# GpSimd's additions wait for the VectorE work that the plan puts ahead of them

## The chip, the cores and the metric

The kernel runs on one core of a Trainium2 chip. The core has five engines that run side by side and meet only through semaphores: TensorE (PE in the profile, PEld for its weight loads), VectorE (DVE), ScalarE (ACT), GpSimd (POOL) and SyncE (SP), which issues most transfers. The metric is the time of one execution on the device, in microseconds (us).

## What is computed

Two stages follow each other. Attention takes 4 batches of 8 heads, 1152 keys and 576 queries (each the mean of two neighbouring ones), 64 wide. A feed-forward layer with a leaky activation follows, 2304 tokens by 512, with 2048 hidden columns.

```python
q_pool = q.reshape(B, H, S // factor, factor, D).mean(axis=3)
scores = scale * np.matmul(q_pool, k.transpose(0, 1, 3, 2))
scores = scores - np.max(scores, axis=-1, keepdims=True)
attn = np.exp(scores)
attn = attn / (np.sum(attn, axis=-1, keepdims=True) + 1e-09)
out = np.matmul(attn, v)
...
h = x @ w_in
g = np.maximum(h, 0.0) + alpha * np.minimum(h, 0.0)
return g @ w_out
```

## The kernel before

**Attention** goes over the heads in 16 pairs (`n` = 0, 2, ... 30). Of a pair, the two heads stand on the two halves of the 128 partitions. The queries are handled in two halves of 288 columns, and for each half the 1152 keys come in nine blocks of 128. For one block TensorE makes the scores of both heads (`scores`, L951: eight matmuls, since q and k are split into a high and a low part, and the negated row maximum is one more product), ScalarE takes the exponential of both (L968) into a tile `p` (named `pa`, 128 x 576), and after the nine blocks TensorE multiplies with the values (`weighted`, L995, 36 records in one run). The row sums need the sum over blocks of the `p` tiles. The nine tiles form two groups, `PARTS[1]` = (0..3) and (4..8), and each group is added up tile by tile at L981. Blocks 6 and 8 (`ADDS[1]`) are added by VectorE, the others by GpSimd; each addition reads two tiles of SBUF and needs the one before it in its group. TensorE then sums over the partitions with a matrix of ones (`sums`, L1017).

While one pair is worked on, TensorE already multiplies q and k of the next (L818 and L825) and VectorE takes the maxima straight out of PSUM (`peaks`, L839, 28 for a pair). VectorE also normalises the results of the pair before (L1054, and L1066 for the low part, twice a pair), makes the low parts of q and k (L691, L699), and converts the weights, which arrive as 64-bit floats (`w_convert`, L409 to L427, and L391).

**The feed-forward layer** uses L479 for all its matmuls: a first sweep over the hidden columns that are ready early (`low_sweep`), and from the end of attention a second over the rest (`high_sweep`).

**The order** of the instructions on each engine is set by a planner, `Scheduler`. Each piece of work is a task with an estimated duration, its needs and a priority; `place` emits the tasks one by one in the planned order of time. Work of VectorE and of GpSimd that has two inputs in SBUF carries `lock=True`: in the plan no two such tasks overlap (`lock_free`), whichever engine they are on. On the chip nothing keeps this. An engine takes its instructions in the planned order and each one waits only for the semaphores of the data that it needs:

```python
if t.lock:
    self.lock_free = at + dur
```

Of the kernel before, what the change touches and what calls it, by code (L numbers as in the profile page):

```python
# [22 lines left out]
PE, ACT, DVE, POOL, SP = range(5)  # L23
# [6 lines left out]
class Buf:  # L30


    def __init__(self, ring=None):
        self.ring, self.t = ring, None
        self.writers, self.users = [], []
        if ring:
            ring.made.append(self)
# [30 lines left out]
class Banks(Ring):  # L68
# [6 lines left out]
    def ready_at(self, place):  # L75
        last = 0
        for bank in place[0]:
            if bank.user is not None:
                for u in bank.user.users:
                    if u.end is None:  # L80
                        return None
                    last = max(last, u.end)
        return last
# [25 lines left out]
class Scheduler:  # L109
# [3 lines left out]
    def __init__(self, col_cost, turn, to_pe, from_pe, slack, dma_fixed):  # L113
        self.tasks, self.ready = [], [[] for _ in range(5)]
        self.free = [0.0] * 5
        self.dma_free = 0.0
        self.now = 0.0
        self.col = 0
        self.lock_free = 0.0
        self.turn = turn  # L120
        self.col_cost, self.to_pe, self.from_pe, self.slack = col_cost, to_pe, from_pe, slack
        self.dma_fixed = dma_fixed
        self.hold = ()

    def add(self, eng, dur, emit, reads=(), writes=(), uses=(), deps=(), prio=0.0, col=0, size=0, kind=None, dma=False, lock=False, fixed=None):
        t = Task()
        t.eng, t.dur, t.emit, t.prio, t.col, t.size, t.kind = eng, dur, emit, prio, col, size, kind
        t.next, t.end, t.avail, t.dma = [], None, None, dma or eng == SP
        t.lock, t.fixed = lock, fixed
        before = set(deps)  # L130
        for b in reads:
            before.update(b.writers)
            b.users.append(t)
        for b in (*uses, *writes):
            b.users.append(t)
        t.takes = [b for b in writes if b.ring is not None]
        for b in writes:
            b.writers.append(t)
        before.discard(t)
        t.deps = list(before)  # L140
        t.left = 0
        for d in t.deps:
            if d.end is None:
                d.next.append(t)
                t.left += 1
        if not t.left:
            self.ready[eng].append(t)
        return t
# [48 lines left out]
    def place(self, at, t):  # L197
        for b in t.takes:
            if b.t is None:
                b.ring.take(b)  # L200
        self.now = at
        t.emit()
        self.ready[t.eng].remove(t)
        dur = t.dur
        if t.eng == PE:
            if t.col != self.col:
                dur += ENTER if t.col else LEAVE
            self.col = t.col
        if t.lock:
            self.lock_free = at + dur  # L210
        self.free[t.eng] = at + dur
        t.end = at + dur
        if t.dma:
            self.dma_free = max(self.dma_free, t.end + 650) + t.size / DMA_RATE
            t.end = self.dma_free
            t.avail = t.end + (self.dma_fixed if t.fixed is None else t.fixed)
        else:
            t.avail = t.end + SYNC
        for n in t.next:
            n.left -= 1  # L220
            if not n.left:
                self.ready[n.eng].append(n)
# [3 lines left out]
def attention_ffn(  # L226
# [87 lines left out]
    nc = tc.nc  # L314
# [15 lines left out]
    def dve(n):  # L330
        return (n + 65) / 0.96

    def act(n, psum=False):
        return n / 1.2 + (50 if psum else 93)
# [13 lines left out]
    DMA_RATE = RATE  # L348
    sch = Scheduler(COL, SF, TO_PE, FROM_PE, (SLP, SLA, SLD, 0, 0), DF)
    add = sch.add  # L350

    def dt(name, shape, dtype):
        return dram.tile(shape, dtype, tag=name, name=name)
# [20 lines left out]
    def w_tiles(f, i, w):  # L374

        if w.ring is None:
            wh[f, i] = hpool[0].tile([P, DMO], F32R, tag=f"wh{f}_{i}", name=f"wh{f}_{i}")
            wl[f, i] = hpool[0].tile([P, DMO], F32R, tag=f"wl{f}_{i}", name=f"wl{f}_{i}")
            return
        flat = flat_of(w, F32R)  # L380
        wh[f, i], wl[f, i] = flat[:, :DMO], flat[:, DMO:2 * DMO]

    def w_split(f, i, mag, prio, ring, left):
        w = Buf(ring)

        def high():
            w_tiles(f, i, w)
            nc.scalar.activation(out=wh[f, i], in_=mag.t, func=AF.Copy)

        def low():  # L390
            nc.vector.tensor_tensor(  # L391
                out=wl[f, i], in0=mag.t, in1=wh[f, i].bitcast(F32), op=ALU.subtract
            )

        t = add(ACT, act(DMO), high, reads=[mag], writes=[w], deps=left, prio=prio)
        add(DVE, dve(DMO), low, reads=[mag], writes=[w], deps=[t], prio=prio, lock=True)
        w_done[f, i] = w

    def w_convert(f, i, prio, release=(), ring=None, left=(), first=()):
        raw, mag, bits = Buf(r_raw), Buf(r_mag), Buf(r_bits)  # L400

        def load():
            nc.sync.dma_start(out=raw.t.rearrange("p n t -> p (n t)"), in_=wt[f, i].bitcast(I32))

        def size():
            nc.scalar.activation(out=mag.t, in_=raw.t[:, :, 1].bitcast(F32), func=AF.Abs)

        def top():
            nc.vector.tensor_scalar(  # L409
                out=bits.t, in0=raw.t[:, :, 1], scalar1=3, scalar2=0x3FFFFFF8,  # L410
                op0=ALU.logical_shift_left, op1=ALU.bitwise_and,
            )

        def tail():
            nc.vector.scalar_tensor_tensor(  # L415
                out=bits.t, in0=raw.t[:, :, 0], scalar=29, in1=bits.t,
                op0=ALU.logical_shift_right, op1=ALU.bitwise_or,
            )

        def sign():  # L420
            nc.vector.scalar_tensor_tensor(
                out=bits.t, in0=raw.t[:, :, 1], scalar=-0x40000000, in1=bits.t,
                op0=ALU.bitwise_and, op1=ALU.bitwise_or,
            )

        def value():
            nc.vector.scalar_tensor_tensor(  # L427
                out=mag.t, in0=mag.t, scalar=F64_TINY, in1=bits.t.bitcast(F32),
                op0=ALU.is_ge, op1=ALU.mult,
            )  # L430

        add(SP, 600, load, writes=[raw], deps=first if f == 0 else (), prio=prio - 1, size=P * DMO * 8)
        t0 = add(ACT, act(DMO), size, reads=[raw], writes=[mag], prio=prio)
        t1 = add(DVE, dve(DMO) * 0.6, top, reads=[raw], writes=[bits], deps=release, prio=prio, lock=True)
        t2 = add(DVE, dve(DMO), tail, reads=[raw], writes=[bits], deps=[t1], prio=prio, lock=True)
        t3 = add(DVE, dve(DMO), sign, reads=[raw], writes=[bits], deps=[t2], prio=prio, lock=True)
        add(DVE, dve(DMO), value, reads=[bits], writes=[mag], deps=[t0, t3], prio=prio, lock=True)
        w_split(f, i, mag, prio, ring, left)

# [639 lines left out]
    with ExitStack() as actx:  # L1079
# [69 lines left out]
        t = add(SP, 600, lambda: nc.sync.dma_start(out=nal, in_=alpha), uses=[], writes=[nal_b], deps=[first_load[0]], prio=3)  # L1149
# [84 lines left out]
```

## Time and profile before

| | |
|---|---|
| median of 3 runs | 842.04 us (840.05 to 842.55) |
| the profiled execution, its time | 839.95 us |
| its span in the profile | 838.2 us |
| TensorE busy (PE) | 825.2 us, 98% |
| VectorE busy | 567.0 us, 68% |
| ScalarE busy | 437.4 us, 52% |
| GpSimd busy | 262.4 us, 31% |
| GpSimd's additions, L981 | 160, 240.5 us |

The shares are averages: attention fills the span to about 440 us, and GpSimd works only there; the second sweep runs from about 501 us to the end.

### The profile page before, as it was taken

To read this page: it belongs to the slowest core of one execution; us is meant where nothing else is said; L and a number is where in the kernel's file an instruction comes from. 1 tells how busy PE (TensorE), PEld (TensorE's weight loads), DVE (VectorE), ACT (ScalarE), POOL (GpSimd) and SP (SyncE) were. 2 spreads that over 40 slices of the span, in tenths; PEclk is the share of its full clock that TensorE was granted. 3 is DMA by queue.
4 is the path that set the end of the run, shared out by engine and by line. 5 is a ranking of instruction groups with operands and counts; after the bars stand their busy time and mean duration, and the time that the engine had idled before them with its cause. 6 is when DMAs were issued, how large, how long until landed. Compare 5 with 4: busy or idle time off the path is not lost.

```text
span 838.2 us, 17447 instructions
## 1 busy us (share of the span) xinstructions
PE 825.2 (98%) x6690; PEld 691.4 (82%) x6690; DVE 567.0 (68%) x1035; ACT 437.4 (52%) x1124; POOL 262.4 (31%) x196
## 2 busy tenths in 40 slices
PE   8999999999999999999999999999999999999997
PEld 8767777676777777776779999998898988988986
DVE  7999999999998988889963799632242232322422
ACT  4657676675766676665754676643232233332321
POOL 5665665565565665654550000000000000000000
PEclk9999999999999999999999999999999999999999
DMA  8234345634354433323233768581330421300301
GB/s 274 58 89 164 82 144 140 197 115 123 87 179 122 122 116 77 83 72 109 69 124 121 248 195 260 177 228 58 91 92 3 120 59 46 91 0 1 91 1 45
DMA packets 67759, 93.71 MB, mean 112 GB/s; under 512 B 20004, under 2 KB 45404, under 8 KB 67676
## 3 DMA queue, kind: packets, MB, share of 16 engines
q1 hardware_dynamic: 65516, 88.18, 33.9%
q0 software_dynamic: 2160, 4.42, 3.6%
q8 instruction: 52, 0.85, 0.4%
q14 instruction: 31, 0.25, 0.1%
HBM read 73.48 MB, written 19.02 MB: 110 GB/s over the span
## 4 chain that ended last, share of the span: by engine, by line
PE 86%; DVE 9%; DMA 2%; issue 1%; ACT 1%; SPq 0%; DVEq 0%; ACTq 0%
PE bank L479 44%; PE bank L951 18%; PE bank L995 15%; PE bank L818 6%; DVE bx L839 3%; PE bank L1017 2%; DMA wraw<-wt 1%; DVE x L1066 1%; DVE pa L981 1%; PE bank L825 1%; PE bank L1129 1%; DMA kk<-kt 1%; DVE pos L515 1%; DVE r L1054 0%; DVE wbits L415 0%
## 5 line engine op out<-in xcount | busy, mean ns | idle before, releaser
L981 POOL TENSOR_TENSOR pa<-pa,pa 128x576 f32<-128x576 f32 x160 | 240.5, 1520 | 155.9 <-ACT pa L968 104.4
L839 DVE TENSOR_REDUCE bx<-bank 128x1 f32<-128x384 f32 (+1 forms) x448 | 214.0, 533 | 22.5 <-PE bank L818 19.9
L968 ACT ACTIVATE pa<-bank 128x288 f32<-128x288 f32 x576 | 199.7, 417 | 25.9 <-PE bank L951 17.4
L951 PE MATMUL bank<-q,k 64*128 64x288 f32 x1728 | 206.2, 311 | 0.8 <-DVE mq L923 0.6
L951 PEld LDWEIGHTS bank<-q,k 64*128 64x128 f32 x1728 | 163.3, 184 | 21.1 <-issue 9.3
L995 PE MATMUL bank<-pa,vv 128*64 128x288 f32 x1152 | 146.8, 409 | 0.0
L995 PEld LDWEIGHTS bank<-pa,vv 128*64 128x64 f32 x1152 | 79.9, 137 | 54.8 <-issue 3.8
L526 DVE TENSOR_TENSOR gw<-gs,gw 128x460 fp32r<-128x460 f32 (+1 forms) x55 | 35.1, 638 | 121.2 <-ACT gw L521 121.2
L951 PE MATMUL bank<-mq,neg 64*128 64x288 f32 x576 | 115.2, 291 | 0.0
L818 PE MATMUL bank<-k,q 64*128 64x384 f32 x384 | 110.1, 362 | 3.5 <-DVE bx L839 2.0
L521 ACT ACTIVATE gw<-gs 128x460 fp32r<-128x460 f32 (+1 forms) x55 | 32.4, 589 | 126.7 <-PE bank L479 115.2
L479 PE MATMUL bank<-wlow,wh 128*128 128x460 f32 (+1 forms) x320 | 93.0, 371 | 0.0
L479 PE MATMUL bank<-gw,wh 128*128 128x460 f32 (+1 forms) x320 | 92.8, 371 | 0.0
L951 PEld LDWEIGHTS bank<-mq,neg 64*128 64x128 f32 x576 | 83.3, 184 | 0.0
L818 PEld LDWEIGHTS bank<-k,q 64*128 64x128 f32 x384 | 62.4, 185 | 16.2 <-DVE bx L839 10.0
L515 DVE SCALAR_TENSOR_TENSOR gs<-gs,nal 128x460 f32<-128x460 f32 (+1 forms) x55 | 38.4, 699 | 52.9 <-ACT gs L510 52.9
L479 PE MATMUL bank<-x,wlow 128*128 128x288 f32 x480 | 66.3, 296 | 0.0
L479 PEld LDWEIGHTS bank<-wlow,wh 128*128 128x128 f32 x320 | 60.0, 188 | 7.1
L479 PE MATMUL bank<-gs,wlow 128*128 128x288 f32 x480 | 65.8, 295 | 0.1
L479 PEld LDWEIGHTS bank<-gw,wh 128*128 128x128 f32 x320 | 60.1, 188 | 6.8
L479 PEld LDWEIGHTS bank<-x,wlow 128*128 128x128 f32 x480 | 64.2, 188 | 1.6 <-issue 1.4
L479 PEld LDWEIGHTS bank<-gs,wlow 128*128 128x128 f32 x480 | 63.9, 188 | 1.4 <-DVE gs L526 0.5
(90 smaller groups left out, 1006.2 us busy)
## 6 DMA issues: line engine op xcount, KB each, us to landing
wraw<-wt SPq DMA_DIRECT2D x32, 512.0 KB
vv<-vt SPq DMA_DIRECT2D x32, 288.0 KB
xs<-x SPq DMA_DIRECT2D x32, 288.0 KB
x<-xs SPq DMA_DIRECT2D x32, 288.0 KB
kk<-kt SPq DMA_DIRECT2D x15, 576.0 KB
r<-rrd SPq DMA_DIRECT2D x64, 72.0 KB
yp<-ys SPq DMA_DIRECT2D x32, 144.0 KB
wlow<-xs SPq DMA_DIRECT2D x16, 288.0 KB
```

Source lines behind the costliest of these rows:

```text
L479: nc.tensor.matmul(out=ps[:, :n], lhsT=w[a, c // DMO][:, c % DMO:c % DMO + P], rhs=lo(hl), start=(first and i == 0), stop=(last and i == 2),)
L515: lambda: nc.vector.scalar_tensor_tensor(out=flat(pos), in0=flat(neg), scalar=nal[:, f:f + 1], in1=flat(pos), op0=ALU.mult, op1=ALU.add),
L521: ACT, act(n), lambda: nc.scalar.activation(out=gs.t[:, 0, :n], in_=flat(pos), func=AF.Copy),
L526: lambda: nc.vector.tensor_tensor(out=gs.t[:, 1, :n], in0=flat(pos), in1=gs.t[:, 0, :n].bitcast(F32), op=ALU.subtract),
L818: nc.tensor.matmul(out=ms.t[:, :JW], lhsT=w.q1.t[d, starts[t]:starts[t] + P], rhs=w.k1.t[d, j * JW:(j + 1) * JW], start=True, stop=True,)
L825: nc.tensor.matmul(out=ms.t[:, :S // 4], lhsT=w.rt.t[d, D - D * u:D - D * u + P], rhs=w.k1.t[d, c:c + S // 4], start=u == 0, stop=u == 1,)
L839: nc.vector.tensor_reduce(out=bx.t[:, at, j:j + 1], in_=ms.t[:, :m], axis=AX.X, op=ALU.max)
L951: nc.tensor.matmul(out=ps.t[i][:, :HQ], lhsT=k.t[d, s] if k else neg[d], rhs=r.t[d, q], start=x == 0, stop=x == len(pairs) - 1,)
L968: lambda ps=ps, p=p, i=i: nc.scalar.activation(out=p.t[:, i], in_=ps.t[i][:, :HQ], func=AF.Exp, scale=SCALE),
L981: lambda a=a, b=p, part=part, e=e: e.tensor_tensor(out=part.t, in0=a.t, in1=b.t, op=ALU.add),
L995: nc.tensor.matmul(out=av.t[i * D:(i + 1) * D, :HQ], lhsT=w.vv[i].t[:, e], rhs=p.t[:, i], start=(e == 0), stop=(e == NC - 1),)
L1017: nc.tensor.matmul(out=ps.t[g * 32:(g + 1) * 32, :HQ], lhsT=ones, rhs=acc[n + g // 2][j].t[:, g % 2], start=j == 0, stop=j == m - 1, tile_ ...
```

## The change

The planner keeps the last VectorE instruction with `lock=True` that it emitted (`port`). When it emits a GpSimd instruction with `lock=True`, it adds a dependence on that one, so that the GpSimd instruction waits for a VectorE semaphore. VectorE gets no wait for GpSimd. The weight conversion's functions now return their instruction, so that they count too. Names, durations and orders in the plan are as before; ten lines are inserted, so L981 is L991 after the change.

```diff
+        self.port, self.after = None, None
...
-        t.emit()
+        made = t.emit()
+        if t.lock and made is not None:
+            if t.eng == DVE:
+                self.port = made
+            elif self.port is not None:
+                self.after(made, self.port)
...
+    sch.after = lambda late, early: tc.add_manual_dep(
+        late.ins, early.ins.name, mybir.DependencyInfo(mybir.DependencyClass.Sync, mybir.DependencyReason.DATA),
+        reason="order on the shared port",
+    )
...
         def low():
-            nc.vector.tensor_tensor(
+            return nc.vector.tensor_tensor(
```

The first place is GpSimd's program in one of the regular pairs (the additions that ran from about 296 to 313 us in the profiled execution). `pa_104<-pa_94,pa_97` adds two tiles of exponentials into a new sum; the brackets name the engines whose semaphores the row waits for. Before:

```order
L981 TENSOR_TENSOR pa_101<-pa_98,pa_99 128x576 [waits Activation_49]
L981 TENSOR_TENSOR pa_101<-pa_101,pa_95 128x576 [waits Activation_49,Pool_49]
L981 TENSOR_TENSOR pa_101<-pa_101,pa_88 128x576 [waits Activation_49,Pool_49]
L981 TENSOR_TENSOR pa_102<-pa_89,pa_90 128x576 [waits Activation_49]
L981 TENSOR_TENSOR pa_102<-pa_102,pa_92 128x576 [waits DVE_49,Activation_49]
L981 TENSOR_TENSOR pa_104<-pa_94,pa_97 128x576 [waits Activation_49]
L981 TENSOR_TENSOR pa_104<-pa_104,pa_100 128x576 [waits Activation_49,Pool_49]
```

The same seven after the change:

```order
L991 TENSOR_TENSOR pa_101<-pa_98,pa_99 128x576 [waits DVE_49,Activation_49]
L991 TENSOR_TENSOR pa_101<-pa_101,pa_95 128x576 [waits Activation_49,Pool_49]
L991 TENSOR_TENSOR pa_101<-pa_101,pa_88 128x576 [waits Activation_49,Pool_49]
L991 TENSOR_TENSOR pa_102<-pa_89,pa_90 128x576 [waits Activation_49]
L991 TENSOR_TENSOR pa_102<-pa_102,pa_92 128x576 [waits DVE_49,Activation_49]
L991 TENSOR_TENSOR pa_104<-pa_94,pa_97 128x576 [waits DVE_49,Activation_49]
L991 TENSOR_TENSOR pa_104<-pa_104,pa_100 128x576 [waits Activation_49,Pool_49]
```

No row moved; the first and the sixth got a wait for VectorE. The sixth waits for this part of VectorE's own program, which is the same before and after (its last instruction, L699, is the one waited for):

```order
L1066 TENSOR_TENSOR x_4110<-r,x_4110 128x288 [waits DMAHW0_49,Activation_49]
L1066 TENSOR_TENSOR x_4114<-r,x_4114 128x288 [waits DMAHW1_49,Activation_49]
L981 TENSOR_TENSOR pa_102<-pa_102,pa_93 128x576 [waits Pool_49]
L691 TENSOR_TENSOR q_4125<-qs,q_3710 128x576 [waits DMASW2_49]
L699 TENSOR_TENSOR k_4135<-kk,k_3756 128x1152
```

Nothing moved there, and VectorE's addition in it still waits for GpSimd.

The second place is the end of attention on GpSimd (about 395 to 418 us), where VectorE also has weights and the first sweep to work on. Before:

```order
L981 TENSOR_TENSOR pa_101<-pa_101,pa_95 128x576 [waits Activation_49,Pool_49]
L981 TENSOR_TENSOR pa_101<-pa_101,pa_88 128x576 [waits Activation_49,Pool_49]
L981 TENSOR_TENSOR pa_102<-pa_89,pa_90 128x576 [waits Activation_49]
L981 TENSOR_TENSOR pa_102<-pa_102,pa_92 128x576 [waits DVE_49,Activation_49]
L981 TENSOR_TENSOR pa_104<-pa_97,pa_100 128x576 [waits Activation_49]
```

After:

```order
L991 TENSOR_TENSOR pa_101<-pa_101,pa_95 128x576 [waits DVE_49,Pool_49]
L991 TENSOR_TENSOR pa_101<-pa_101,pa_88 128x576 [waits DVE_49,Pool_49]
L991 TENSOR_TENSOR pa_102<-pa_89,pa_90 128x576 [waits DVE_49]
L991 TENSOR_TENSOR pa_102<-pa_102,pa_92 128x576 [waits DVE_49,Activation_49]
L991 TENSOR_TENSOR pa_104<-pa_97,pa_100 128x576 [waits DVE_49]
```

Here all five in a row wait for VectorE, and where ScalarE's name went away, the VectorE instruction itself stands behind that piece of ScalarE's work.

## Rows read from the trace of the kernel before

**Rows 1.** Busy us of each engine (instructions) in two stretches; then PEclk, DMA share, GB/s.

```profile
200.00:250.00 50.00, 48.76 (x497) 35.37 (x497) 48.69 (x88) 32.19 (x91) 28.19 (x21) 1.00 0.44 130
250.00:300.00 50.00, 50.00 (x540) 38.13 (x537) 42.55 (x85) 33.60 (x94) 30.20 (x23) 1.00 0.38 109
```

**Rows 2.** The chain that ended last, in order of time: start us, us, what.

```profile
58.17 4.52 PE bank L995 x36
...
72.17 1.59 DVE x L1066
...
84.72 4.52 PE bank L995 x36
...
109.88 4.52 PE bank L995 x36
...
123.20 1.96 DVE x L1066 x2
...
135.51 4.54 PE bank L995 x36
...
148.88 2.04 DVE x L1066 x2
...
161.59 4.52 PE bank L995 x36
...
187.12 4.52 PE bank L995 x36
...
202.55 2.15 DVE x L1066 x2
204.70 1.88 DVE pa L981
...
214.67 4.59 PE bank L995 x36
...
290.21 4.52 PE bank L995 x36
...
315.07 4.52 PE bank L995 x36
...
382.28 1.90 DVE pa L981
...
473.44 5.34 DMA wraw<-wt
```

**Rows 3.** L479 alone in a stretch: busy us (instructions) of PE and PEld.

```profile
50.00:380.00 330.00, 0.00 (x0) 0.00 (x0) 1.00 0.41 118
```

**Rows 4.** Timeline of VectorE, 300 to 312 us: start us, us, instructions.

```profile
305.01 2.23 DVE L1066 TENSOR_TENSOR x<-r,x 128x288 fp32r<-128x288 f32 x2
307.17 0.75 DVE L981 TENSOR_TENSOR pa<-pa,pa 128x576 f32<-128x576 f32 x1
...
308.51 1.34 DVE L699 TENSOR_TENSOR k<-kk,k 128x1152 fp32r<-128x1152 f32 x1
```

**Rows 5.** Timeline of GpSimd, 300 to 322 us; idle time before a row in brackets.

```profile
303.94 2.99 POOL L981 TENSOR_TENSOR pa<-pa,pa 128x576 f32<-128x576 f32 x2 [1.85 <-ACT k L684]
310.28 4.32 POOL L981 TENSOR_TENSOR pa<-pa,pa 128x576 f32<-128x576 f32 x3 [3.35 <-ACT pa L968]
```

**Rows 6.** Groups of VectorE's instructions by line, 440 to 838 us: busy us, mean ns.

```profile
L1066 DVE TENSOR_TENSOR x<-r,x 128x288 fp32r<-128x288 f32 x2 | 0.9, 458 | 0.3 <-ACT x L1061 0.2
```

**Rows 7.** The same view of VectorE, 20 to 250 us.

```profile
L839 DVE TENSOR_REDUCE bx<-bank 128x1 f32<-128x384 f32 (+1 forms) x267 | 127.3, 533 | 5.8 <-PE bank L818 4.3 <-PE bank L825 0.6
```

**Rows 8.** What TensorE waited for, 50 to 250 us: us in total, times, longest.

```profile
PE bank L818 <- DVE bx L839: 1.7, 3, 0.7
```

**Rows 9.** The same, 370 to 440 us.

```profile
PE bank L1017 <- DVE pa L981: 1.1, 1, 1.1
```

**Rows 10.** Timeline of GpSimd, 393 to 440 us.

```profile
401.58 3.28 POOL L981 TENSOR_TENSOR pa<-pa,pa 128x576 f32<-128x576 f32 x2 [1.42 <-ACT pa L968]
412.32 14.84 POOL L981 TENSOR_TENSOR pa<-pa,pa 128x576 f32<-128x576 f32 x9 [7.46 <-DVE pa L981]
```

More of the change, by code (lines that the diff above doesn't have):

```diff
@@ L408, in top @@
         def top():
-            nc.vector.tensor_scalar(
+            return nc.vector.tensor_scalar(
                 out=bits.t, in0=raw.t[:, :, 1], scalar1=3, scalar2=0x3FFFFFF8,
@@ L414, in tail @@
         def tail():
-            nc.vector.scalar_tensor_tensor(
+            return nc.vector.scalar_tensor_tensor(
                 out=bits.t, in0=raw.t[:, :, 0], scalar=29, in1=bits.t,
@@ L420, in sign @@
         def sign():
-            nc.vector.scalar_tensor_tensor(
+            return nc.vector.scalar_tensor_tensor(
                 out=bits.t, in0=raw.t[:, :, 1], scalar=-0x40000000, in1=bits.t,
@@ L426, in value @@
         def value():
-            nc.vector.scalar_tensor_tensor(
+            return nc.vector.scalar_tensor_tensor(
                 out=mag.t, in0=mag.t, scalar=F64_TINY, in1=bits.t.bitcast(F32),
```

## Prediction

> **What bounds the kernel now.** I read the busy times by stretch first. From 200 to 250 us TensorE is busy 48.76 of 50 us and VectorE 48.69; from 250 to 300 us TensorE is busy all 50 and VectorE 42.55 [rows 1]. So TensorE is the bound, but in the first half of attention VectorE runs level with it and now and then holds it up. In neither is GpSimd near full (28.19 and 30.20).
>
> The chain in order of time shows where VectorE holds TensorE up. The run of 36 value matmuls (L995) comes twice a pair, so I take one start a pair as a clock: 58.17, 84.72, 109.88, 135.51, 161.59, 187.12, 214.67, then 290.21 three pairs on, and 315.07 [rows 2]. The last step, 24.86 us, is a pair that TensorE alone bounds. All pairs here hold the same matmuls, for nothing of the first sweep runs between 50 and 380 us [rows 3]. The steps before are longer by 1.69, 0.30, 0.77, 1.22, 0.67 and 2.69 us, and the three to 290.21 (75.54 us) by 0.96 together: 8.3 us in all. That is the most that a freer VectorE can give there.
>
> What makes VectorE late is in the same rows. L1066 takes 0.458 us where GpSimd is idle [rows 6]; on the chain one costs 1.59, and pairs of them 1.96, 2.04 and 2.15 instead of 0.92. An L981 of VectorE costs 1.88 and 1.90 [rows 2] instead of 0.75 [rows 4]. These are collisions: the instruction has begun but stands until a GpSimd addition is through, which takes 4.32/3 = 1.44 us [rows 5]. The maxima do not collide: 267 of them average 0.533 us in the stretch where GpSimd is busy more than half the time [rows 7], and one that stood behind an addition would show over 1.
>
> **What the change removes.** Each step of it that costs or gives something:
>
> 1. In a regular pair GpSimd's second addition of the two that end at 306.93 [rows 5] starts among VectorE's two L1066 (2.23 us instead of 0.92 from 305.01 on) and then VectorE still has L981, L691 and L699 to do, to 308.51 + 1.34 = 309.85 [rows 4]. After the change this addition waits for L699. What follows L699 on VectorE are maxima, which do not collide, so the addition runs beside them. VectorE's collision of about 2.23 - 0.92 = 1.3 us goes away but for the 0.2 us or so by which the first L1066 still meets the addition before, so about 1.1.
>
> 2. The addition itself then starts near 309.85 - 1.1 = 308.75 instead of before 306.93 - 1.4, some 3.2 us later, and ends near 310.2. GpSimd's next addition started at 310.28 after 3.35 us of idle time, since it waits for ScalarE [rows 5]. So the delay costs nothing as long as VectorE does lose its collision: the idle time covers it. Without that cover it would end at 311.3, 1.0 us late. Queued behind it are the next additions and a query load on GpSimd's queue; TensorE's row sums and a free `pa` tile wait for these.
>
> 3. In the steady pairs nothing comes of it, because TensorE is the bound there [rows 1]. It counts where VectorE is on the chain. I give each pair the smaller of its collisions and its excess over 24.86: the pair from 58.17 has 1.59 - 0.46 = 1.13 (excess 1.69), so 1.13; the one from 109.88 has 1.96 - 0.92 = 1.04, but an excess of 0.77 only; that from 135.51 has 2.04 - 0.92 = 1.12; that from 187.12 has 2.15 - 0.92 + 1.88 - 0.75 = 2.36; the others have no collision on the chain: 0. Together 5.4 us [rows 2].
>
> 4. At 382.28 the row sums wait for a collided L981 (1.90 - 0.75 = 1.15); TensorE stood idle 1.1 us for it [rows 9]. That 1.1 goes too.
>
> 5. The new waits themselves: where one binds, it is counted in step 2. For one that is already fulfilled the nearest row is the three additions from 310.28, the last two of which carry two waits each and still follow every 1.44 us [rows 5]. So I take 0; if one cost 0.1 us, two or three in a pair would take 0.3 us of an engine that is idle some 20 of 50 us [rows 1], which hides it. No transfer, no matmul and no order changes.
>
> **The sum**: 5.4 + 1.1 = 6.5 us. From below, what is certain to be VectorE's doing is TensorE's own idle time: 1.7 us for maxima from 50 to 250 us [rows 8] and 1.1 later, 2.8 together. From above it is all excess, 8.3 + 1.15 = 9.45. I take 6.5, since the chain names the collided instructions one by one and pipelined matmuls hide part of a stall from the idle time. The profiled execution took 839.95 us, so it would come to 833.5, and 830.5 to 837.2 by the bounds. The three runs shown have a median of 842.04, 2.1 above; the profiled one is the fastest of the four. I add 0.5 for that: 834.0.
>
> **A rule weighed against this.** The Trainium skill, in "SBUF — State Buffer", "Who interferes with whom", says that VectorE and GpSimd share a pair of ports as an exclusive lock, that whoever issues first has it for the whole instruction, that a VectorE instruction with two SBUF inputs contends with a GpSimd one that reads SBUF, and that `tensor_reduce` on trn2 never does. The trace agrees: 1.9 us against 0.75, and 0.533 for the maxima. By the same rule a lock only changes hands: what VectorE no longer waits, someone else must, and a moved addition can meet the next VectorE instruction. That is the first rival.
>
> **Rivals.**
>
> *The collision only moves (or the gain is given back).* VectorE gets no wait for GpSimd, so an addition that is let go late can stand in the way of VectorE instructions behind the one it waited for. Then VectorE loses the same 1.1 us a little later and the sum is 0: about 840 to 841.5. For it: in the first half weight conversions lie between the maxima and will be hit now and then. Against it: of 230 us in that stretch 127.3 are maxima [rows 7], and the plan puts the additions over these. A second way to the same end: the weight loads are on the chain later (5.34 us at 473.44 [rows 2]); if their start did not move forward with attention, the gain would end there. I think it does, since they follow instructions that move too.
>
> *The held additions make things late.* Each pair has a held addition; if VectorE runs as late as before, GpSimd falls 1.0 us behind (step 2), VectorE's own addition of that group waits for it, and all maxima queue behind. Over 15 pairs this is 15 us: 855, or 848 with the gain kept. It decides where an addition is held more than the idle time behind it (3.35 us in the steady pair) beyond its old start plus VectorE's recovery. The end of attention is nearest: five in a row wait there, with 7.46 us of idle time after 401.58 + 3.28 = 404.86 [rows 10]. Against it: ScalarE, which fills the `pa` tiles, is what GpSimd itself waits for in most of its idle time.
>
> *The change does nothing*, because the waits were already implied by the data: excluded for the additions shown, which ran before the instruction they will wait for; I put it with the first rival.
>
> **How the numbers follow.** My forecast (a gain of 2.8 to 9.5 us on the profiled run): 0.74. Collision moves or the gain is given back: 0.15. Late additions: 0.08. A larger gain, if VectorE's head start also takes pairs below 24.86 us: 0.03. A measurement of this kernel can tell about 0.3%, 2.5 us, as the three runs show. Faster by more than that: 0.77, from the forecast (0.72 of its 0.74) and the larger gain, and a little of the rest. Within: 0.15. Slower: 0.08. The forecast alone gives 830.5 to 837.2; to leave no more than 2 in 10 out, the range goes to 840.5, into the first rival, and down to 830.
>
> **What the profile after would show.** If right: L1066 near 0.5 us on average, as in [rows 6]; no L981 of VectorE over 1.5 us at 204 or 382; the six steps of the L995 clock before 214 us, 156.5 us together, down to about 151, and the last unchanged at 24.86; VectorE less busy from 50 to 250 us; GpSimd's idle time put down to VectorE instead of ScalarE. Step 2 is wrong if TensorE or ScalarE waits for GpSimd's L981. The first rival shows as collisions that move to L421, L427, L391 and L415 with the total unchanged. The prediction fails if pairs keep their 25.5 us although the collisions are gone: then something else than the port made VectorE late.

## The result and the profile after

The changed kernel took 831.35 us (median of 5 runs, 830.55 to 833.7), the kernel before, on the same chip, 840.53 us (5 runs, 839.66 to 842.55): a ratio of 0.989, with a 95% interval of 0.9873 to 0.9906, so 9.2 us less. The forecast was 834.0, with a range of 830.0 to 840.5.

The profiled execution after is the longest of its five, 833.7 us with a span of 831.9; it and one more (833.0) had a mean granted clock of 0.997, the other three (830.55 to 831.35) one of 0.998 or 0.999. Its page, busy time by engine and then the chain by engine:

```profile
PE 820.7 (99%) x6690; PEld 691.5 (83%) x6690; DVE 545.4 (66%) x1035; ACT 437.2 (53%) x1124; POOL 250.4 (30%) x196
...
PE 91%; DMA 3%; DVE 3%; ACT 1%; issue 1%; SPq 0%; POOL 0%; DVEq 0%; ACTq 0%; POOLq 0%
```

VectorE has fallen from 9% of the chain to 3%, and TensorE has risen from 86% to 91%. Groups by line, over the whole span, with the idle time ahead of each:

```profile
L991 POOL TENSOR_TENSOR pa<-pa,pa 128x576 f32<-128x576 f32 x160 | 228.7, 1449 | 174.9 <-ACT pa L978 58.0 <-DVE k L709 24.7 <-DVE wbits L425 13.3
...
L991 DVE TENSOR_TENSOR pa<-pa,pa 128x576 f32<-128x576 f32 x64 | 50.2, 784 | 15.5 <-POOL pa L991 15.5
...
L1076 DVE TENSOR_TENSOR x<-r,x 128x288 fp32r<-128x288 f32 x32 | 15.3, 511 | 1.4 <-ACT x L1071 1.1
```

L1076 is the old L1066: 511 ns on average instead of 990, near the 458 ns that it takes where GpSimd is idle [rows 6]. ScalarE's exponentials were named for 104.4 us of GpSimd's idle time before and are for 58.0 now; most of the rest now stands against VectorE's instructions. Busy time by stretch (PE, PEld, DVE, ACT, POOL, then the granted clock):

```profile
20.00:25.00 5.00, 3.41 (x39) 2.66 (x39) 5.00 (x10) 4.31 (x11) 4.59 (x3) 1.00 0.72 178
25.00:30.00 5.00, 5.00 (x45) 4.42 (x42) 3.93 (x9) 3.51 (x10) 2.04 (x2) 0.66 0.00 0
...
200.00:250.00 50.00, 49.99 (x529) 37.33 (x527) 47.85 (x94) 34.14 (x99) 29.60 (x22) 1.00 0.45 130
250.00:300.00 50.00, 50.00 (x539) 38.51 (x537) 41.23 (x85) 34.18 (x94) 30.43 (x23) 1.00 0.39 109
```

From 200 to 250 us TensorE is busy 49.99 us instead of 48.76 [rows 1]. The first two stretches show a loss at the start, told below. The chain in order of time:

```profile
33.85 4.54 PE bank L1005 x36
...
60.40 4.51 PE bank L1005 x36
...
71.98 0.64 PE bank L961 x8
72.89 4.52 PE bank L1005 x36
...
86.06 4.52 PE bank L1005 x36
...
110.36 4.52 PE bank L1005 x36
...
135.29 4.56 PE bank L1005 x36
...
160.44 4.52 PE bank L1005 x36
...
185.38 4.52 PE bank L1005 x36
...
210.92 4.59 PE bank L1005 x36
...
285.73 4.52 PE bank L1005 x36
...
310.43 4.52 PE bank L1005 x36
...
359.84 4.52 PE bank L1005 x36
...
389.16 4.51 PE bank L1005 x36
...
426.11 4.52 PE bank L1005 x36
```

Four starts of the same clock before, which [rows 2] do not have:

```profile
31.23 4.58 PE bank L995 x36
...
364.81 4.52 PE bank L995 x36
...
395.40 4.52 PE bank L995 x36
...
432.69 4.52 PE bank L995 x36
```

The value matmuls (L1005, before L995) are the clock again; the collided L1066 ahead of the second of them [rows 2] is gone, TensorE's own work stands there. The first run starts at 33.85, 2.62 us later than before (31.23). From there on it gains: at 60.40 it is 2.23 us later than before, at 135.29 0.22 earlier, at 210.92 3.75, at 285.73 4.48, at 310.43 4.64, and at 426.11 6.58 (before 432.69). From its first value matmuls on, attention thus won 2.62 + 6.58 = 9.2 us. The medians differ by as much, the two profiled executions (839.95 and 833.7) by 6.25 only: the late start took the difference back.

Two timelines, each by the windows that the text speaks of. VectorE:

```profile
21.19 2.03 DVE L1162 TENSOR_SCALAR nal<-nal 128x16 f32<-128x16 f32 x1
...
300.53 1.02 DVE L1076 TENSOR_TENSOR x<-r,x 128x288 fp32r<-128x288 f32 x2
301.48 0.74 DVE L991 TENSOR_TENSOR pa<-pa,pa 128x576 f32<-128x576 f32 x1
...
302.81 1.34 DVE L709 TENSOR_TENSOR k<-kk,k 128x1152 fp32r<-128x1152 f32 x1
```

And GpSimd:

```profile
21.47 3.19 POOL L991 TENSOR_TENSOR pa<-pa,pa 128x576 f32<-128x576 f32 x2
...
299.45 1.41 POOL L991 TENSOR_TENSOR pa<-pa,pa 128x576 f32<-128x576 f32 x1 [1.83 <-ACT k L694]
304.30 5.82 POOL L991 TENSOR_TENSOR pa<-pa,pa 128x576 f32<-128x576 f32 x4 [3.43 <-DVE k L709]
...
400.62 1.42 POOL L991 TENSOR_TENSOR pa<-pa,pa 128x576 f32<-128x576 f32 x1 [1.86 <-DVE pos L525]
403.84 1.41 POOL L991 TENSOR_TENSOR pa<-pa,pa 128x576 f32<-128x576 f32 x1 [1.80 <-DVE gs L536]
```

This is the regular pair of [rows 4] and [rows 5], 4.5 us earlier. The two L1076 take 1.02 us instead of 2.23. The held addition starts at 304.30, as soon as L709 is through (302.81 + 1.34), and three more follow it without a gap. At the end of attention the additions are let go one by one.

### The profile page after: what moved, and what is told of

Same layout as the page of the kernel before. It is cut to its first block, busy times and chain, and to the rows that moved or that the text cites. A ratio compares the mean times of both kernels' runs of the same rounds, so it can differ in the third digit from the quotient of the medians.

```text
span 831.9 us, 17471 instructions
## 1 busy us (share of the span) xinstructions
PE 820.7 (99%) x6690; PEld 691.5 (83%) x6690; DVE 545.4 (66%) x1035; ACT 437.2 (53%) x1124; POOL 250.4 (30%) x196
## 4 chain that ended last, share of the span: by engine, by line
PE 91%; DMA 3%; DVE 3%; ACT 1%; issue 1%; SPq 0%; POOL 0%; DVEq 0%; ACTq 0%; POOLq 0%
PE bank L489 42%; PE bank L961 21%; PE bank L1005 17%; PE bank L828 6%; PE bank L1027 2%; DMA wraw<-wt 2%; PE bank L835 1%; DMA kk<-qt 1%; DVE pos L525 1%; PE bank L1139 1%; DMA x<-xs 1%; DVE wbits L425 0%; DVE bx L849 0%; DVE gs L536 0%; DVE wmag L437 0%
## 5 line engine op out<-in xcount | busy, mean ns | idle before, releaser
L991 POOL TENSOR_TENSOR pa<-pa,pa 128x576 f32<-128x576 f32 x160 | 228.7, 1449 | 174.9 <-ACT pa L978 58.0
L1005 PE MATMUL bank<-pa,vv 128*64 128x288 f32 x1152 | 146.8, 409 | 0.0
L1005 PEld LDWEIGHTS bank<-pa,vv 128*64 128x64 f32 x1152 | 79.9, 137 | 54.9 <-issue 3.8
L828 PE MATMUL bank<-k,q 64*128 64x384 f32 x384 | 107.4, 359 | 1.7 <-ACT k L766 1.3
```

The lines of the kernel that those rows point to most:

```text
L828: nc.tensor.matmul(out=ms.t[:, :JW], lhsT=w.q1.t[d, starts[t]:starts[t] + P], rhs=w.k1.t[d, j * JW:(j + 1) * JW], start=True, stop=True,)
L991: lambda a=a, b=p, part=part, e=e: e.tensor_tensor(out=part.t, in0=a.t, in1=b.t, op=ALU.add),
L1005: nc.tensor.matmul(out=av.t[i * D:(i + 1) * D, :HQ], lhsT=w.vv[i].t[:, e], rhs=p.t[:, i], start=(e == 0), stop=(e == NC - 1),)
```

## The experiments

**The theory:** the gain is VectorE's, which no longer stands behind GpSimd's additions; each place at which it did gives its part. **The rivals:** the gain comes from one place alone or from the weight conversions; any order between the two engines would do; without the change's wait a collision that is taken away only moves to the next instruction. The kernel before was timed again beside the experiments, on the same chip each time: 840.73 us for the first four below (15 runs), 839.67 for the one with two instructions freed and for the last (9 runs), 840.05 for the other four (23 runs). The value-matmul clock is given relative to the trace of before, plus for later and minus for earlier.

**Where the gain lies: the wait on the first 91 of GpSimd's instructions only (up to about 240 us).**

```diff
-            elif self.port is not None:
-                self.after(made, self.port)
+            else:
+                self.held += 1
+                if self.port is not None and self.held <= 91:
+                    self.after(made, self.port)
```

> The waits stand only on GpSimd's first 91 two-input instructions, those up to about 241 us of the profile before; the rest run as before. Theory (the gain is VectorE no longer standing behind GpSimd in the pairs where VectorE holds TensorE up, 8.3 of it before 290 us and 1.15 near 382): all but about 1.2 us of the gain stays, so 832 to 833.5 against 840.5 before, and the chain has the collided L981 near 382 back. Rival (the gain comes from the end of attention, where five additions in a row are held, or from GpSimd being held anywhere, evenly over the pairs): about half the gain, 836.

834.36 us (834.02 to 835.45), ratio 0.9928 (0.9914 to 0.9941); 832 to 833.5 was missed, since the rest is worth more than the 1.2 us put down for it. The clock goes from +0.1 to -6.3 us at 240 us and then stays at -6.3 to the end. The profile shows TensorE's wait for VectorE's sum (now L1030, of [rows 9]) again, 1.1 us. So 6.4 us are won in the first half of attention, one us more than the terms of the sum for it, and nothing is lost later.

**The other part, `self.held > 91`.**

> The waits stand only on the additions after the 91st, from about 246 us on. Theory: the pairs from 250 to 370 us are bound by TensorE at 24.86 us and gain nothing although their L1066 collisions go; 1.2 us is won near 382; so 839 to 839.7 against 840.5. Rival (held additions help every pair): 836 or less, and steps of the L995 clock under 24.8 us.

837.83 us (837.39 to 839.73), ratio 0.9971 (0.9961 to 0.998). 839 to 839.7 was missed. From 2.2 us late the clock stays nearly flat to 250 us (+2.1) and then gains: 0.9 by 365 us, in small steps of 0.1 to 0.3 a pair, 1.3 at 382, 0.3 at the end, to -0.4. That is 2.6 us, about twice what was expected: the steady pairs gain too, with steps of 24.7 us, as the rival had it. By the medians the two halves won 6.4 and 2.9 us, 9.3 together, and the whole change 9.2. The parts add up, so the gain is not at one place.

**The weight conversions not counted:** their five functions return nothing again, so no addition waits for one.

```diff
-            return nc.vector.scalar_tensor_tensor(
+            nc.vector.scalar_tensor_tensor(
```

> The five instructions of the weight conversion are not tracked, so additions wait only for VectorE's work of attention and of the first sweep (L1066, L691, L699, L981 and so on). Theory: the additions that met L1066 still wait for L699 or L1066 and the L1066 collisions stay away; additions let go earlier meet the conversion run behind (about 1.2 us each in perhaps half of the nine early pairs, hidden in part): 7 of the 9 us stay, 832 to 834.5. Rival (the long waits for conversion instructions, up to 5.9 us, carry the gain): 836 to 839.

833.32 us (832.51 to 834.37), ratio 0.9914 (0.9899 to 0.993): 7.4 of the 9.2 us stay. L1076 still averages 512 ns, so the waits that free it are those on q, k and the normalising. GpSimd's additions take 1480 ns instead of 1449. The waits on the conversions account for some 2 us, if for anything: the intervals of the two ratios overlap.

**The other direction: VectorE waits for GpSimd's last such instruction, GpSimd for nothing.**

```diff
-            if t.eng == DVE:
-                self.port = made
-            elif self.port is not None:
-                self.after(made, self.port)
+            if t.eng != DVE:
+                self.pool = made
+            elif self.pool is not None:
+                self.after(made, self.pool)
```

> The opposite dependence alone: a two-input VectorE instruction waits for the last such GpSimd instruction ahead of it in the plan; GpSimd is not held. Theory (what costs is GpSimd starting ahead of its place, which this does not prevent): the L1066 collisions stay, mean of L1066 near 1 us, and VectorE, with the maxima behind it, also waits for additions that are late: no gain, 840 to 846. Rival (any fixed order on the port helps, whoever waits): 833 to 837.

844.58 us (843.37 to 847.03), ratio 1.0053 (1.0036 to 1.007): slower. VectorE's groups:

```profile
L1077 DVE TENSOR_TENSOR x<-r,x 128x288 fp32r<-128x288 f32 x32 | 29.0, 940 | 2.4 <-POOL pa L992 2.1 <-ACT x L1072 0.2
...
L438 DVE SCALAR_TENSOR_TENSOR wmag<-wmag,wbits 128x512 f32<-128x512 f32 x32 | 21.8, 685 | 3.7 <-POOL pa L992 2.9 <-ACT wmag L417 0.4
```

The normalising (L1077) collides as before, 940 ns, since GpSimd still starts ahead of its place, and VectorE now has idle time for GpSimd on top. So a wait of VectorE alone doesn't pay: it leaves the collisions in place, and TensorE's work behind VectorE comes later still.

**Without the change, one collision taken away:** L1066 made an operation with one input, so the kernel leaves out the subtraction.

```diff
-                lambda r=r, x2=x2: nc.vector.tensor_tensor(
-                    out=x2.t[:, 1], in0=r.t, in1=x2.t[:, 0].bitcast(F32), op=ALU.subtract
+                lambda r=r, x2=x2: nc.vector.tensor_reduce(
+                    out=x2.t[:, 1], in_=r.t.unsqueeze(2), axis=AX.X, op=ALU.max
```

> The kernel before, without any new wait; L1066 is a reduction over an axis of one element instead of the subtraction of two tiles, so it leaves out the subtraction (the low part of attention's result is then a copy), has the same place and size and one input in SBUF. Theory (the cost is two-input VectorE instructions that stand behind a GpSimd addition that started among them): without holding GpSimd at all, L1066 takes about 0.4 us, and of the 9.2 us some 4.5 to 7 are won (L1066's collisions, without those of L981 and of the conversions): 834 to 836 against 840.7. Rival (the gain needs GpSimd to be held, by pacing it or by keeping it from other things): 839.5 or more.

838.24 us (836.62 to 841.15), ratio 0.9978 (0.9962 to 0.9994); 834 to 836 was missed. VectorE's groups:

```profile
L981 DVE TENSOR_TENSOR pa<-pa,pa 128x576 f32<-128x576 f32 x64 | 62.2, 971 | 6.3 <-POOL pa L981 6.3
...
L1066 DVE TENSOR_REDUCE x<-r 128x288 fp32r<-128x288 f32 x32 | 13.0, 440 | 0.0
```

L1066 is free (440 ns), but L981 behind it rises from 890 to 971 ns: part of the collisions moved one instruction on, and L691 rises from 820 to 1085. The clock wins 4.9 us to 395 us (+2.4 to -2.5) and gives 1.5 back at the end of attention (-1.0), where the chain shows two L415 of 1.84 and 1.80 us and two L421 of 1.85 and 1.83. The twelve times spread over 4.5 us, so the size of the gain is uncertain. The steady pairs gain here too:

```profile
313.27 4.52 PE bank L995 x36
...
337.96 4.52 PE bank L995 x36
```

That step is 24.69 us where the kernel before has 24.86, and no addition is held.

**Both taken away, still without the change's waits:** L1066 as above, and VectorE's share of L981 with one input as well, so the kernel also leaves out that share of the row sums; alpha's sign moved to ScalarE (below).

```diff
-                    lambda a=a, b=p, part=part, e=e: e.tensor_tensor(out=part.t, in0=a.t, in1=b.t, op=ALU.add),
+                    (lambda b=p, part=part: nc.vector.tensor_reduce(out=part.t, in_=b.t.unsqueeze(3), axis=AX.X, op=ALU.max)) if eng == DVE else
+                    (lambda a=a, b=p, part=part, e=e: e.tensor_tensor(out=part.t, in0=a.t, in1=b.t, op=ALU.add)),
```

> The kernel before without any new wait, alpha's sign on ScalarE, and both L1066 and VectorE's own L981 as reductions with one input: so it leaves out the low part of attention's result and VectorE's share of the row sums, in the same places and sizes. With L1066 alone freed the collisions had gone over to L981 (mean 971 ns, 890 before). Theory (what costs is VectorE standing behind GpSimd): L1066 and L981 near 0.45 and 0.7 us, the collisions left go to L691, L699 and the conversions, the chain of attention gains 6 to 8 us against the kernel with alpha's sign on ScalarE alone (841.96), so 834 to 836, with GpSimd held nowhere. Rival (GpSimd must be held): as with L1066 alone, 838 or more.

834.93 us (833.66 to 836.36), ratio 0.9941 (0.9928 to 0.9955). VectorE's groups:

```profile
L981 DVE TENSOR_REDUCE pa<-pa 128x576 f32<-128x576 f32 x64 | 47.4, 741 | 7.2 <-POOL pa L982 7.2
...
L1067 DVE TENSOR_REDUCE x<-r 128x288 fp32r<-128x288 f32 x32 | 13.0, 443 | 0.0
...
L691 DVE TENSOR_TENSOR q<-qs,q 128x576 fp32r<-128x576 f32 x15 | 16.6, 1105 | 0.0
```

With no addition held, two instruction kinds that no longer stand behind additions give 4.7 us against the kernel before, and more against the same kernel without the two edits, which is told last but one (841.96 us on another chip; 7.0 by the medians, 5.6 by the two ratios). So the collisions of these two kinds are the cause of about half of the 9.2 us or more; part of the rest has moved to L691 (1105 ns, where it takes 751 in the next experiment).

**Both directions: GpSimd waits for VectorE and VectorE for GpSimd.**

```diff
+                if self.pool is not None:
+                    self.after(made, self.pool)
...
+                self.pool = made
```

> Both dependences: GpSimd waits as in the change, and a two-input VectorE instruction also waits for the last such GpSimd instruction ahead of it in the plan, so that no two overlap. Theory (VectorE no longer sets TensorE's pace after the change, so its last 10 to 15 us of collisions are worth nothing, and waits of VectorE for late additions hold the maxima up): 831 to 836, not faster than the change. Rival (what collisions are left still cost): 828 to 830.

834.22 us (831.75 to 835.03), ratio 0.9916 (0.9896 to 0.9936). VectorE's groups:

```profile
L996 DVE TENSOR_TENSOR pa<-pa,pa 128x576 f32<-128x576 f32 x64 | 47.9, 748 | 13.5 <-POOL pa L996 13.4
...
L1081 DVE TENSOR_TENSOR x<-r,x 128x288 fp32r<-128x288 f32 x32 | 13.4, 453 | 4.3 <-POOL pa L996 4.0 <-ACT x L1076 0.2
```

Here the mean of every such instruction is the undisturbed one, so nothing collides, and still it is not faster than the change (ratios 0.9916 and 0.989). The collisions that the change leaves cost nothing that a wait of VectorE could win back.

**Alpha's sign on ScalarE, with the change.** This is for the late start, 2.03 us of `nal` at 21.19.

```diff
-            DVE, 100,
-            lambda: nc.vector.tensor_scalar(
-                out=nal, in0=nal, scalar1=-1.0, scalar2=0.0, op0=ALU.mult, op1=ALU.add
-            ),
+            ACT, 100,
+            lambda: nc.scalar.activation(out=nal, in_=nal, func=AF.Copy, scale=-1.0),
```

> The change, and the sign of alpha is set by ScalarE in place of the VectorE instruction L1162 (16 columns), which took 2.03 us in the profile after instead of 0.35, with TensorE idle 1.59 us behind it and the granted clock at 0.66 from 25 to 30 us. Theory (that instruction, which carries no lock, stood behind GpSimd's first additions): the start comes out as in the profile before, the L995 clock begins near 31.2 instead of 33.85, and the runs come to 830 to 831.3 without those at 833. Rival (the stall is due to the query load that came late): as the change, 831.4, with the first clock step still late in some runs.

831.3 us (830.79 to 831.46), ratio 0.9884 (0.9865 to 0.9904). Its stretch of 25 to 30 us:

```profile
25.00:30.00 5.00, 5.00 (x63) 4.58 (x62) 4.85 (x12) 4.20 (x14) 2.80 (x2) 1.00 0.00 1
```

The clock starts at +0.2 instead of +2.6 and ends at -9.4. The median is that of the change, so the late start seems not to weigh on the change's median; the runs lie within 0.7 us of each other instead of 3.2.

**The same without the change.**

> The kernel before with that one instruction on ScalarE and nothing else. Theory (the gain of the change has nothing to do with it): 839.5 to 840.7, the first L995 step at 31.2. Rival (it meets GpSimd in the kernel before as often as after): 838.5.

841.96 us (840.5 to 843.18), ratio 1.0008 (0.9993 to 1.0024): no difference that is clear of noise, though the median lies above the 839.5 to 840.7 expected. The profiled execution starts at +0.5, and between 84.6 and 96.8 us loses another 2.0. The timelines of VectorE and GpSimd there:

```profile
87.25 2.48 DVE L391 TENSOR_TENSOR wlow<-wmag,wlow 128x512 fp32r<-128x512 f32 x1
...
87.46 1.71 POOL L981 TENSOR_TENSOR pa<-pa,pa 128x576 f32<-128x576 f32 x1
```

In the trace of before the same L391 took 0.67 us, and GpSimd's additions from 86.97 took 9.15 us for four: there VectorE had the port and GpSimd stood. In that trace L391 began 0.38 us ahead of GpSimd's addition, here 0.21, since VectorE had waited 0.35 us for ScalarE just before it instead of 0.17. In the kernel with L1066 alone freed it is 0.39 and L391 takes 0.67 us; in that with both freed (which has alpha's sign on ScalarE too) it is 0.21 again and L391 takes 2.46. So in these four kernels, none of which has the change's waits, 0.2 us more or less of a head start goes with 1.8 us of L391.

**The change once more.**

> The change itself once more, beside the run with alpha's sign on ScalarE (831.3). Theory: 831 to 833.7, some runs with the late start, none below 830.5; rival (the late start of the profiled run is the recording's): all near 831.3 but the profiled one.

830.86 us (830.09 to 832.73), ratio 0.989 (0.9875 to 0.9905), as the first time; the lowest is under the 830.5 expected. The profiled execution is again the longest. Its clock starts 1.0 us late, without a slow `nal`, and ends at -7.1.

## Why the prediction was right, and where not

**The bound and the mechanism: right.** VectorE held TensorE up through two-input instructions that stood behind additions; semaphores are thus not the only place where these two engines meet. The experiment with two kinds of VectorE instruction freed wins 4.7 us or more with no wait at all, and that with VectorE waiting loses.

**Step 1, the regular pair: right.** Two L1076 at 300.53 take 1.02 us, 1.2 less; 1.1 was forecast.

**Step 2, the held addition costs nothing: right.** It was to start near 308.75 and end near 310.2; in the new trace it starts at 304.30, which is 308.8 with the 4.5 us added that the pair is earlier. What TensorE and VectorE waited for, by engine, after (the weight loads from 50 to 250 us, the others over the span):

```profile
PEld bank L828 <- DVE bx L849: 2.8, 12, 0.5
...
POOL pa L991 <- ACT pa L978: 58.0, 24, 5.3
POOL pa L991 <- DVE k L709: 24.7, 7, 5.0
...
DVE pa L991 <- POOL pa L991: 15.5, 11, 3.0
```

TensorE and ScalarE wait for no addition of GpSimd. VectorE's own additions wait more (15.5 us instead of 7.4), the longest near the end of attention, where the chain is TensorE's.

**Step 3, the sum over the pairs: mis-sized.** The four pairs named were to give 1.13, 0.77, 1.12 and 2.36 us and gave, from the starts in the chain, 0.89, 0.70, 0.93 and 2.01: 4.5 instead of 5.4. But "the others have no collision on the chain: 0" is where it failed: the pairs from 84.72 and 161.59 gained 0.86 and 0.59, the three up to 290.21 0.73 together, and the steady pair, "a pair that TensorE alone bounds", 24.86 - 24.70 = 0.16. The pairs that were given 0 made up 2.2 us to 290.21 alone. Nor was 24.86 a floor: the step from 86.06 is 24.30. The reason lies beside the view that was used. TensorE was put down as busy, but its weight loads waited. In the trace of before, from 50 to 250 us, then from 250 to 370 us:

```profile
PEld bank L818 <- DVE bx L839: 6.6, 21, 1.0
...
PEld bank L1017 <- DVE pa L981: 2.6, 4, 1.0
...
PEld bank L1017 <- DVE pa L981: 2.4, 5, 0.5
PEld bank L1017 <- POOL pa L981: 1.8, 4, 0.4
```

Of these the first is 2.8 after the change (above); the others are gone, though from 250 to 370 us the same loads then wait 2.2 us for nothing that the profile names, 0.4 before. A busy share of 50 of 50 us hid these waits. That the small gains of the steady pairs come from exactly them is argued, not shown. That they come from the collisions is shown: the steady step is 24.7 us where the late additions alone are held and also where nothing is held but L1066 has one input, and 24.87 us (283.93 to 308.80) where only the early additions are held.

**Step 4, 382 us: right.** 1.1 us was forecast; the step from 364.81 to 395.40 was 30.59 us and is 29.32 after, so 1.3, and 1.3 in the late part alone.

**Step 5, the waits themselves: nothing seen.** In the regular pair three additions that carry waits follow the held one without a gap.

**The sum** was 6.5 us and 9.2 were measured, near the upper bound of 9.45. By the clock, 6.9 us came between 58 and 315 us, where the sum had 5.4; 1.9 after 315, where it had 1.1; and 0.4 before 58, where it had nothing. That the two profiled executions differ by 6.25 us, close to 6.5, is luck: the late start hid the rest. The lower bound of 2.8 counted TensorE's idle time alone and was far off, for the same reason as step 3. The 0.5 added for the runs shown was about right: the median before is 840.53, 0.6 above the profiled execution.

**What the profile after was to show:** L1066 near 0.5 us (511 ns); no long L981 at 204 or 382 (0.74 at 201.82, 0.75 at 376.18); the six steps down from 156.5 to about 151 (60.40 to 210.92 is 150.5); VectorE less busy from 50 to 250 us (189.47 us, 193.42 before); GpSimd idle for VectorE. All this came, but the last step was not "unchanged at 24.86".

**The rivals.** *The collision moves:* a little. From 20 to 250 us L701 (the old L691) rose from 871 to 924 ns, but L437 fell from 942 to 801; without the change's waits it moves, as L981 and L691 show in two experiments. *Late additions:* TensorE shows none, at the end of attention neither. The slower case came with the wait on the other engine only. *A larger gain* was given 0.03, on the condition that pairs fall below 24.86 us. They did (24.30, 24.70), and 9.2 us is just inside the forecast's 9.5.

## What to carry to other kernels

Where a plan treats a resource of two engines as exclusive, let the chip keep it, with a wait on the engine that has time (GpSimd, 30% busy); the same wait on the other cost 0.5%. Before a stretch is given 0 because TensorE is busy throughout, read what its weight loads wait for. And mark every instruction that takes the port: freeing one kind moves part of its collisions to the next, and an unmarked one stays exposed.

## What the runs showed that was not expected

**A tiny instruction can take two microseconds.** `nal`, 16 columns with one input in SBUF and no `lock`, took 0.35 us before and 2.03 us after (21.19), while GpSimd's additions ran from 21.47. The maxima behind it came late, and TensorE stood idle for 1.59 us at 23.4. The Trainium skill, "SBUF — State Buffer", "Who interferes with whom", counts `tensor_scalar` among the operations that can enter a mode with two ports and then contend with GpSimd; the 2.03 us fit that. That the additions hold it is not shown otherwise. Of eight profiles of changed kernels that leave `nal` on VectorE six show 1.86 us or more, one of them without any held addition (L1066 alone freed), and two not (0.36), one of these of the very change. So it is a draw, and not the work of the change's waits. Moved to ScalarE, `nal` takes 0.22 us.

**The granted clock followed in four of the six.** In the change it was 0.66 from 25 to 30 us, a mean between the two levels of 1.2 and 2.4 GHz, after TensorE had been busy 3.41 of the 5 us before; with both, the first value matmuls came 2.62 us late. In the experiment without the conversions `nal` was as slow (1.9 us) and TensorE idle for 1.5 us, but the clock stayed at 1.00 and the start was 0.9 us late. What decides between the two is open.

**Which of the two stands can't be read from their starts.** Of the same two instructions at 87 us GpSimd stood where VectorE was 0.38 or 0.39 us ahead (two kernels), and VectorE where it was 0.21 ahead (two others). The Trainium skill, in the same section, has it that the order of issue decides who blocks; here VectorE began first in all four and still stood in two, so the start that the trace shows is not yet that order. `nal` says the same: with GpSimd's addition starting 0.28 or 0.29 us behind it, it was quick in the kernel before and in two others, and slow in four. Why GpSimd sometimes gets the port between two VectorE instructions that follow each other closely, and sometimes waits through several, was not settled.
